# Chunked attention and a gated feed-forward block: copies of v shared between two engines, and two more tiles transposed by DMA

## The chip, the cores and the metric

The kernel runs on one core of a Trainium2 chip. A core has a matrix engine (TensorE, PE in the profile; its weight loads are PEld), a vector engine (VectorE, DVE), an activation engine (ScalarE, ACT), a general one (GpSimd, POOL) and a synchronising one (SyncE, SP), each with a queue of its own that it works through in order. POOL, SP and ACT also issue DMA transfers, which all run on the same 16 DMA engines. Engines wait for each other through semaphores. On-chip memory is SBUF, and matrix products land in PSUM. The metric is the time of one execution on the device in microseconds (us), lower is better.

## The reference: what is computed

Attention over 4 batches, 8 heads, 768 positions and a head size of 64. The positions go in chunks of 32 queries. Each chunk sees 8 memory keys, 16 positions to its left, its own 32 and 8 to its right, 64 keys in all, with a softmax over them. The heads' results are put side by side as rows of 512, and a feed-forward block follows:

```python
for c in range(nc):                       # 24 chunks of 32 queries
    k_full = concat([mem_k, k[l_start:r_end]])
    v_full = concat([mem_v, v[l_start:r_end]])
    a = softmax(scale * q_c @ k_full.T)
    out[chunk] = a @ v_full
x = out as (3072, 512)
y = (relu(x @ w_gate) * (x @ w_val)) @ w_out     # 512 -> 1536 -> 512
```

## The kernel before, in words

**Tiles.** The 3072 rows are 24 tiles of 128 rows, six a batch, each with four chunks. `BLOCKS` gathers the tiles into feed-forward blocks of 2, 2, 2, 4, 4, 4, 4 and 2.

**A tile's attention.** q and k come in by POOL's loads (L254), cast to bf16, into a ring of 18 buffers. They are transposed on PE (`qk_t`, L275) and copied out of PSUM (`qk_copy`), or, for tiles from `LATE_QK` on, by transposing DMA transfers that SP issues (`qk_transfer`, L283): q lands where it is used, k lands in `k_t` and is copied from there into `kT`, where every chunk's keys have the batch's memory keys beside them. Then follow the scores (L309, for which also the next tile's k must be in place), maximum, subtraction, exponent, sum, reciprocal and normalisation (L322 to L352; the exponent on ACT, all else on DVE), the transposition of the probabilities P, on PE (`p_t`, L358) with a copy, or, for tiles from `LATE_P` on, by a transposing transfer from SP (`p_transfer`, L362), the product with v (`values`, L388; L374 and L381 in batch 0), and a copy into the block's xT (`x_copy`).

**v.** For batches 1 to 3, v lies in `v_bd`, two sets used in turn: for each chunk 56 rows of v and 8 of memory, in blocks that are zero elsewhere. POOL loads 32 rows a chunk for each half of the heads (L185). The remaining 24, the upper slots, are the first rows of the next chunk and are copied on chip from one partition group to another: `upper`, 16 copies a batch of 24 x 768 elements, all on DVE (L81, `v_bd<-v_bd`). Rows of memory values come by small transfers (L168), the zeros by ops named `z1` and `z0` on ACT and DVE.

**Feed-forward.** For each block and each of 12 slices of 128 hidden columns: four products for the gate and four for the value (`first`, L407), a relu on ACT (`relu`, L413), a multiplication on DVE (`gate`, L419). Four PSUM buffers are used in turn. Then, per tile, 12 products with w_out (`second`, L432), a copy and a store (`store`, L439).

**The order of the work.** Nothing is scheduled at run time: a planner in the kernel's Python (`schedule`, L682) plays the work through with a cost for each op, and each engine's queue is filled in the order that results. An op has the engines that may do it with a cost on each, its dependencies, a priority tuple (lower is first) and resources that it takes and gives. Whenever an engine is free, in the order POOL, PE, ACT, DVE, SP, the planner walks through that engine's ops by priority and takes the first that is ready. Relus and gates have priority 0, attention ops 1 with the tile's number behind it, feed-forward products 2, some zeroing 3. An `up` op has (1, 6b-1, 9) or (1, 6b+2, 9) for batch b: behind all of tile 6b-1's (or 6b+2's) ops, ahead of the next tile's. Attention ops on PE also keep a margin of 0.4 us (`MARGIN`) behind what they depend on.

For the transposing transfers the planner counts `ISSUE` 1.4 us on SP (and 0.08), then `LAND` 4.5 us for q and k or `LAND_P` 3.0 us for P; a transfer of q or k is put 1.0 us (`SLACK`) behind the landing of its load. The q and k transposes on PE are paced by the feed-forward products (`pace`, from `marks`); those by transfer are paced by the scores of six tiles before (`pace_t`). A transfer issued while the load queue is busy puts that queue 1.1 us back in the plan.

**Memory keys.** `new_batch` (L259) takes one of two q/k buffer sets and fills the memory keys of a batch into all its chunks, one copy on DVE (L263). It stands at tile 6b-2, after that tile's q has been transposed.

Of the kernel before, what the change touches and what calls it, by code (L numbers as in the profile page):

```python
# [14 lines left out]
ACT = mybir.ActivationFunctionType  # L15
# [4 lines left out]
def kernel(  # L20
# [23 lines left out]
    TPB = S // 128  # L44
# [8 lines left out]
    BAND0 = 48  # L53
    UT = 3

    LATE_QK, LATE_P = 15, 15

    KEY_RUNS = ((0, CH, 0), (KW, 64, CH), (CH, KW, CTX))
    assert sum(BLOCKS) == NT and NMEM == 8 and D == 64 and H == 8
# [130 lines left out]
    def upper(b, par, i0, i1, eng):  # L190

        x = v_bd[b % NSET].rearrange("p h c d -> p (h c) d")
        d = slice(D * par, D * par + D)
        copy(eng, x[64 * par + CH:64 * par + CTX, i0:i1, d], x[64 * par:64 * par + CTX - CH, i0 + 1:i1 + 1, d])
# [64 lines left out]
    def new_batch(b):  # L259
        qT[b] = kvpool.tile([128, HP, S], BF16, name="qT")  # L260
        kT[b] = kvpool.tile([128, HP, NCH, KW], BF16, name="kT")
        src = kmemT[:, b]
        nc.vector.tensor_copy(  # L263
            kT[b][:, :, :, 16:16 + NMEM],
            bass.AP(tensor=src.tensor, offset=src.offset,
                    ap=[src.ap[0], [NMEM, HP], [0, NCH], [1, NMEM]]))
# [180 lines left out]
    ops, loads = {}, []  # L447
# [3 lines left out]
    def op(key, eng, fn, deps=(), prio=(0,), take=(), give=(), after=()):  # L451
        ops[key] = dict(eng=eng, fn=fn, deps=list(deps), prio=prio, take=list(take), give=list(give),
                        after=list(after))
# [31 lines left out]
    op("vm0", {"DVE": 0.5}, lambda e: nc.vector.tensor_copy(vmem_0, vmem_f), [("vml", 1.8)], prio=(1, 0, 4.5))  # L485
    for b in range(B):
        op(("new", b), {"DVE": 0.4}, lambda e, b=b: new_batch(b), ["kmc"], take=["kv"],
           prio=(-4.5,) if b == 0 else (1, TPB * b - 2, 0), after=[("t", TPB * b - 2, 0)] if b else [])


    seq = [(blk, m) for g0, g1 in GROUPS for blk in range(2) for m in range(g0, g1)]
# [28 lines left out]
    for a in range(NT):  # L520
        b, t = divmod(a, TPB)
# [60 lines left out]
    for rank, (blk, m) in enumerate(seq):  # L582
        n = BLOCKS[blk]
# [34 lines left out]
    for b in range(1, B):  # L618
        for n in range(2 * HP):
            hp, par = divmod(n, 2)  # L620
            for m in range(TPB // UT):
                i0 = NCH * hp + 4 * UT * m
                i1 = min(i0 + 4 * UT, HP * NCH - 1)
                op(("up", b, n, m), {"DVE": 0.1 + 64 * 0.5e-3 * (i1 - i0)},
                   lambda e, b=b, par=par, i0=i0, i1=i1: upper(b, par, i0, i1, engine[e]),
                   [("vl", b, par)], (1, TPB * b - 1 + UT * m, 9), (), (), [("v", TPB * b - 7)] if b > 1 else [])

# [51 lines left out]
    def timed(d):  # L679
        return isinstance(d, tuple) and len(d) == 2 and isinstance(d[1], float)  # L680

    def schedule():  # L682
        done, started, times = {}, set(), [0.7]
        free = {e: 0.7 for e in ("PE", "ACT", "DVE", "SP", "POOL")}
        queue_end, flying, gives = 0.0, [], [(WARM + 0.15, "fps")]
        room["fps"] -= 1
        heapq.heappush(times, WARM + 0.15)
        todo = {e: [] for e in free}
        order, n_load = [], 0
        names = lambda o: [d[0] if timed(d) else d for d in o["deps"]] + o["after"]  # L690
        missing = {k: len(set(names(o))) for k, o in ops.items()}
        users = {}
        for k, o in ops.items():
            for d in set(names(o)):
                users.setdefault(d, []).append(k)

        def offer(k):
            for e in ops[k]["eng"]:
                bisect.insort(todo[e], (ops[k]["prio"], k), key=lambda x: x[0])

        for k in ops:
            if not missing[k]:
                offer(k)

        def ready(o, t, margin=0.0):
            if any(d not in started for d in o["after"]):
                return False
            for d in o["deps"]:
                d, lag = d if timed(d) else (d, 0.0)
                if d not in done or done[d] + lag + margin > t + 1e-9:  # L710
                    return False
            return all(room[r] >= o["take"].count(r) for r in o["take"])

        while len(started) < len(ops) + len(loads):
            t = heapq.heappop(times)
            while times and times[0] <= t + 1e-9:
                heapq.heappop(times)
            for g in [g for g in gives if g[0] <= t + 1e-9]:
                gives.remove(g)
                room[g[1]] += 1  # L720
            flying = [f for f in flying if f > t]
            moved = True
            while moved:
                moved = False
                for e in ("POOL", "PE", "ACT", "DVE", "SP"):
                    if free[e] > t + 1e-9:
                        continue
                    if e == "POOL":
                        if n_load == len(loads):
                            continue  # L730
                        o = loads[n_load]
                        if len(flying) >= 8 or not ready(o, t):
                            continue
                        n_load += 1
                        key = o["key"]
                        if o["n"]:
                            end = t + 0.62 + 0.27e-3 * o["n"]
                            queue_end = max(queue_end, end + 0.8) + o["work"]
                            flying.append(queue_end + 1.0)
                            done[key] = queue_end + (1.2 if n_load < 8 else 2.4 if n_load < 45 else 6.0 if key[0] == "vl" else 4.0)  # L740
                        else:
                            end = done[key] = t + max(o["work"], 0.6)
                        fn = o["fn"]
                    else:
                        o = None
                        for _, key in todo[e]:
                            late_pe = e == "PE" and t > 36.0 and ops[key]["prio"][0] == 1
                            if ready(ops[key], t, MARGIN if late_pe else 0.0):
                                o = ops[key]
                                break  # L750
                        if o is None:
                            if e == "PE" and 1.3 < t < WARM:
                                order.append((t, lambda: idle_product(256)))
                                free[e] = t + (0.213 if t < 9.0 else 0.11)
                                heapq.heappush(times, free[e])
                            elif e == "PE" and t <= 1.3:
                                heapq.heappush(times, 1.31)
                            continue
                        for x in o["eng"]:
                            todo[x].remove((o["prio"], key))  # L760
                        d = o["eng"][e]
                        d, lat = d if isinstance(d, tuple) else (d, d)
                        d *= (1.8 if e == "PE" and t < 8.0 and key[0] in ("t", "p", "sh", "f") else 1.0)
                        end = t + d
                        done[key] = end + 0.25 if e == "PE" else t + lat + 0.08

                        if queue_end > t:
                            queue_end += 1.1 if e == "SP" and key[0] in ("t", "pc") else 0.7 if key[0] == "oc" else 0.0
                        fn = lambda o=o, e=e: o["fn"](e)
                        for g in o["give"]:  # L770
                            g, lag = g if isinstance(g, tuple) else (g, 0.0)
                            gives.append((done[key] + lag, g))
                            heapq.heappush(times, done[key] + lag)
                    for r in o["take"]:
                        room[r] -= 1
                    started.add(key)
                    for k in users.get(key, ()):
                        missing[k] -= 1
                        if not missing[k]:
                            offer(k)  # L780
                    order.append((t, fn))
                    free[e] = end
                    for x in (end, done[key], done[key] + 0.2, done[key] + 1.5, done[key] + MARGIN):
                        heapq.heappush(times, x)
                    moved = True
            assert times, [k for k in ops if k not in started][:20]
        return order

    for _, fn in schedule():
        fn()  # L790
# [30 lines left out]
```

## Time and profile before

| | us |
|---|---|
| median of 3 runs | 245.17 (244.69 to 246.42) |
| profiled execution | 246.7 |
| its span | 244.9 |
| PE busy | 235.3 |
| DVE busy | 154.0 |
| ACT busy | 122.0 |
| POOL busy | 77.7 |
| copies of v's upper slots on DVE, 48 | 18.3 |

The span runs from the first to the last instruction of the program that the profiler recorded. A timeline line has the start in us from the span's start, the duration, the engine, the line of the kernel (L79 and L81 are the helper `copy`, on ACT and DVE), the operation, and the tile written, an arrow, the tiles read; "x4" counts instructions that were merged; a bracket gives the idle time of the engine just before and what ended it. Instructions of one engine overlap at their ends, so that the step from start to start is the time that one costs its queue. Two engines' names with a q (SPq, ACTq, POOLq) stand for the part that issues transfers. A table by windows gives each engine's busy time in a stretch.

### The profile page before, as it was taken

The numbers are of one execution on the slowest core, as the hardware profiler recorded it, in microseconds if no ns is written. First come the engines' busy times: TensorE is split into PE (matmuls) and PEld (weight loads), VectorE is DVE, ScalarE is ACT, GpSimd is POOL, SyncE is SP. The second block draws the span as 40 slices with busy tenths as digits, with TensorE's granted clock in tenths as the row PEclk, the third lists the DMA queues.
The fourth block names the chain that finished last, engine by engine and source line by source line (L and its number), as shares of the span: only waits on it lengthen the run. The fifth ranks groups of instructions, "written<-read, shape, count | busy, mean of one in ns | idle before, by whom it ended". The sixth has DMA issues, their size and how long they took to land.

```text
span 244.9 us, 6549 instructions
## 1 busy us (share of the span) xinstructions
PE 235.3 (96%) x2706; PEld 140.5 (57%) x2706; DVE 154.0 (63%) x313; ACT 122.0 (50%) x271; POOL 77.7 (32%) x102
## 2 busy tenths in 40 slices
PE   7898999999889999899999999999999999999994
PEld 4576887884379644454544544554445444444873
DVE  5664867977979649988648999995432034310430
ACT  7577778693365336755335655354331233312432
POOL 8975679215984099038250000000000000000000
PEclk9999999999999999999999999999999999999999
DMA  6999999999999999999993121443001210002102
GB/s 71 172 178 203 201 163 151 185 130 124 195 180 169 90 139 119 113 159 128 109 226 60 35 42 29 133 122 48 0 0 45 86 43 0 3 35 93 45 0 86
DMA packets 96413, 25.17 MB, mean 103 GB/s; under 512 B 87424, under 2 KB 93312, under 8 KB 96384
## 3 DMA queue, kind: packets, MB, share of 16 engines
q0 software_dynamic: 76128, 14.65, 85.9%
q1 hardware_dynamic: 16656, 3.82, 15.2%
q10 hardware_dynamic: 3600, 6.29, 7.4%
q8 instruction: 21, 0.34, 0.7%
q14 instruction: 8, 0.07, 0.1%
HBM read 28.55 MB, written 6.29 MB: 142 GB/s over the span
## 4 chain that ended last, share of the span: by engine, by line
PE 63%; DMA 18%; DVE 8%; POOL 5%; issue 3%; ACT 2%; ACTq 0%; POOLq 0%; DVEq 0%
PE out_ps L432 21%; PE g_ps L407 19%; PE v_ps L407 18%; DMA v_bd<-in_v_dram 8%; DMA qk_p<-in_q_dram 6%; DMA w_gate_sb<-in_moe_w_gate_dram 4%; DVE v_bd L81 3%; PE xT_ps L388 2%; PE s_ps L309 1%; DVE gvT L419 1%; POOL v_n L199 1%; DVE dif L329 1%; POOL qk_p L227 1%; DVE mx L322 1%; PE pT_ps L358 1%
## 5 line engine op out<-in xcount | busy, mean ns | idle before, releaser
L419 DVE TENSOR_TENSOR gvT<-v_ps,g_relu 128x256 f16<-128x256 f32 (+1 forms) x96 | 52.8, 553 | 55.5 <-PE v_ps L407 40.4
L407 PE MATMUL v_ps<-xT,w_val_sb 128*128 128x256 f16 (+1 forms) x384 | 78.2, 326 | 0.0
L407 PE MATMUL g_ps<-xT,w_gate_sb 128*128 128x256 f16 (+1 forms) x384 | 78.1, 326 | 0.0
L413 ACT ACTIVATE g_relu<-g_ps 128x256 f16<-128x256 f32 (+1 forms) x96 | 46.8, 490 | 50.3 <-PE g_ps L407 49.1
L432 PE MATMUL out_ps<-w_out_sb,gvT 128*128 128x512 f16 (+2 forms) x300 | 66.0, 371 | 0.0
L407 PEld LDWEIGHTS <-w_gate_sb 128*128 128x128 f16 x384 | 36.3, 98 | 23.7
L407 PEld LDWEIGHTS <-w_val_sb 128*128 128x128 f16 x384 | 36.0, 98 | 21.7 <-issue 0.2
L432 PEld LDWEIGHTS <-gvT 128*128 128x128 f16 x300 | 27.9, 98 | 29.5
L79 ACT COPY o_sb<-out_ps 128x512 f32<-128x512 f32 (+2 forms) x25 | 14.2, 568 | 36.6 <-PE out_ps L432 28.5
L337 ACT ACTIVATE p_exp<-dif 128x256 f16<-128x256 f32 (+2 forms) x72 | 19.6, 337 | 11.9 <-DVE dif L329 11.4
L81 DVE COPY v_bd<-v_bd 24x768 f16<-24x768 f16 (+1 forms) x48 | 18.3, 423 | 3.8 <-DMA v_bd<-in_v_dram 3.3
L254 POOL DMA_DIRECT2D qk_b<-in_q_dram x18 | 16.3, 904 | 8.9 <-DMA v_bd<-in_v_dram 5.7
L322 DVE TENSOR_REDUCE mx<-s_ps 128x8 f32<-128x512 f32 x24 | 16.5, 686 | 4.1 <-PE s_ps L309 3.6
L254 POOL DMA_DIRECT2D qk_b<-in_k_dram x18 | 16.3, 904 | 5.4 <-DMA w_out_sb<-in_moe_w_out_dram 4.0
L341 DVE TENSOR_REDUCE sm<-p_exp 128x8 f32<-128x512 f16 x24 | 16.3, 678 | 2.0 <-ACT p_exp L337 1.9
L352 DVE TENSOR_TENSOR p_n<-p_exp,rinv 128x512 f16<-128x512 f16 x24 | 16.5, 686 | 0.3
L329 DVE TENSOR_TENSOR dif<-s_ps,mx 128x512 f32<-128x512 f32 x24 | 16.4, 682 | 0.2
L168 POOL DMA_DIRECT2D v_bd<-vmem x16 | 10.5, 664 | 14.5 <-DMA v_bd<-in_v_dram 13.1
L185 POOL DMA_DIRECT2D v_bd<-in_v_dram x12 | 11.0, 928 | 11.4 <-DVE gvT L419 10.6
L79 ACT CAST xT<-xT_ps 128x512 f16<-128x512 f32 x16 | 9.4, 584 | 8.2 <-PE xT_ps L388 6.5
L388 PEld LDWEIGHTS <-v_bd 128*128 128x128 f16 x288 | 9.8, 96 | 4.0 <-DVE v_bd L81 0.7
L141 PE MATMUL idle_ps<-idle 128*128 128x256 bf16 x69 | 10.7, 302 | 1.1 <-DVE warm L475 1.1
(56 smaller groups left out, 170.7 us busy)
## 6 DMA issues: line engine op xcount, KB each, us to landing
out_dram<-o_sb ACTq DMA_DIRECT2D x23, 256.0 KB
qk_b<-in_k_dram POOLq DMA_DIRECT2D x18, 128.0 KB, 7.5
qk_b<-in_q_dram POOLq DMA_DIRECT2D x18, 128.0 KB, 7.5
v_bd<-in_v_dram POOLq DMA_DIRECT2D x6, 384.0 KB, 12.5
w_out_sb<-in_moe_w_out_dram POOLq DMA_DIRECT2D x2, 768.0 KB, 11.5
qk_p<-in_k_dram POOLq DMA_DIRECT2D x3, 256.0 KB, 5.4
qk_p<-in_q_dram POOLq DMA_DIRECT2D x3, 256.0 KB, 6.8
v_n<-in_v_dram POOLq DMA_DIRECT2D x6, 128.0 KB, 6.5
```

Source lines behind the costliest of these rows:

```text
L79: nc.scalar.copy(o, i)
L81: eng.tensor_copy(o, i)
L254: nc.gpsimd.dma_start(qk_b[a, i], bass.AP(tensor=x.tensor, offset=x[b, 0, 128 * t, 0].offset, ap=[[D, 128], [S * D, H], [1, D]]))
L322: nc.vector.reduce_max(SM[a, "mx"], s4, axis=AX.X)
L329: nc.vector.tensor_tensor(out=SM[a, "dif"].rearrange("p (m r) a s -> p r m a s", r=2), in0=S_ps.pop(a).rearrange("p r (m a) s -> p r m a s ...
L337: nc.scalar.activation(p[:, :, :, s0:s0 + k1 - k0], dif[:, :, :, k0:k1], ACT.Exp, scale=SCALE)
L341: nc.vector.reduce_sum(SM[a, "sm"], SM[a, "p"], axis=AX.X)
L352: nc.vector.tensor_tensor(out=P_n[a], in0=SM.pop((a, "p")), in1=rinv_b, op=ALU.mult)
L407: nc.tensor.matmul(ps, lhsT=w[:, f, 128 * m:128 * m + 128], rhs=xTs[blk][:, f, :], start=(f == 0), stop=(f == NFC - 1))
L413: nc.scalar.activation(st["r", m], st.pop((0, m)), ACT.Relu)
L419: nc.vector.tensor_tensor(out=st["gv"][:, m, :], in0=st.pop((1, m)), in1=st.pop(("r", m)), op=ALU.mult)
L432: nc.tensor.matmul(st["o", t, c], lhsT=st["gv"][:, m, 128 * t:128 * t + 128], rhs=w_out_sb[:, m, c[0]:c[1]], start=(m == 0), stop=(m == ND ...
```

## The change

Five edits:

- `LATE_QK` and `LATE_P` go from 15 to 13, so that q, k and P of tiles 13 and 14 are transposed by transfers from SP. The k tiles pass through `k_t` and a copy from SBUF.
- The `up` ops may run on ACT (cost 0.16 us + 0.9 ns x 64 for each chunk) as well as on DVE (0.1 us + 0.55 ns x 64, where it was 0.5).
- The planner, as it walks through an engine's ops, notes whether an op of higher priority that is not ready would be ready 0.3 us later (`soon`). If so and the first ready op is an `up` or a `z0`, the engine takes nothing at that moment.
- `new_batch` for batches 2 and 3 may stand from the scores of tile 6b-5 on, with priority (1, 6b-5, 8). Batch 1 keeps its place.
- With tiles 13 and 14 no longer transposed on PE, their q and k are paced by the scores of tiles 7 and 8 and not by the feed-forward products.

```diff
-    LATE_QK, LATE_P = 15, 15
+    LATE_QK, LATE_P = 13, 13
...
         op(("new", b), {"DVE": 0.4}, lambda e, b=b: new_batch(b), ["kmc"], take=["kv"],
-           prio=(-4.5,) if b == 0 else (1, TPB * b - 2, 0), after=[("t", TPB * b - 2, 0)] if b else [])
+           prio=(-4.5,) if b == 0 else (1, TPB * b - 2, 0) if b == 1 else (1, TPB * b - 5, 8), after=[("t", TPB * b - 2, 0) if b == 1 else ("s", TPB * b - 5)] if b else [])
...
-                op(("up", b, n, m), {"DVE": 0.1 + 64 * 0.5e-3 * (i1 - i0)},
+                op(("up", b, n, m), {"ACT": 0.16 + 64 * 0.9e-3 * (i1 - i0), "DVE": 0.1 + 64 * 0.55e-3 * (i1 - i0)},
...
                         o = None
+                        soon = False
                         for _, key in todo[e]:
                             late_pe = e == "PE" and t > 36.0 and ops[key]["prio"][0] == 1
                             if ready(ops[key], t, MARGIN if late_pe else 0.0):
-                                o = ops[key]
+                                o = None if soon and key[0] in ("up", "z0") else ops[key]
                                 break
+                            soon = soon or ready(ops[key], t + 0.3)
```

## The prediction

> **What bounds the kernel now.** I read the page's busy times and slices first, then the PE timeline, then the waits, then SP's and DVE's timelines around the tiles that the change touches.
>
> ```profile
> PE 235.3 (96%) x2706; PEld 140.5 (57%) x2706; DVE 154.0 (63%) x313; ACT 122.0 (50%) x271; POOL 77.7 (32%) x102
> ...
> DMA  6999999999999999999993121443001210002102
> ```
>
> PE is busy in 96% of the span at a granted clock of 1.00. Matmuls overlap in the records, so I checked by start to next start: four 512-column products of the feed-forward part start 0.86 to 0.87 us apart in the last 60 us and in most groups before. From 25 us on PE runs work that has to be done, with few holes; the end moves by what leaves PE's queue and by the holes that open or close. DMA is full (nine tenths) to slice 22, about 135 us, and almost empty after.
>
> The holes are few. The table of windows gives PE 12.24 of 14.00 us in 60:74 and 25.23 of 26.00 in 87:113, and a full count in the other stretches from 25 to 240: 1.76 + 0.77 = 2.53 us in all. In the PE timeline:
>
> ```profile
> 100.19 0.55 PE L388 MATMUL xT_ps<-pT,v_bd 128*128 128x32 f16 x16
> 100.60 0.38 PE L275 MATMUL qk_ps<-ident_b,qk_b 128*128 128x128 bf16 x4
> 100.82 1.03 PE L407 MATMUL v_ps<-xT,w_val_sb 128*128 128x512 f16 x4
> 102.62 0.38 PE L275 MATMUL qk_ps<-ident_b,qk_b 128*128 128x128 bf16 x4 [0.78 <-ACT xT L79]
> 102.84 1.03 PE L407 MATMUL g_ps<-xT,w_gate_sb 128*128 128x512 f16 x4
> ...
> 117.10 0.38 PE L358 MATMUL pT_ps<-band,p_n 128*128 128x128 f16 x4
> 117.32 1.46 PE L432 MATMUL out_ps<-w_out_sb,gvT 128*128 128x512 f16 x6
> ```
>
> The reader sees that a group of four transposes takes 0.22 us to the next start, and that the hole of 0.78 us stands in front of one. By the order of tiles (L275 comes twice a tile, k one tile ahead) that one is tile 13's k; 117.10 is tile 13's P. The holes of 60:74 (0.42, 1.04, 0.30) come from DVE:
>
> ```profile
> 59.40 1.57 DVE L81 COPY v_bd<-v_bd 24x768 f16<-24x768 f16 x4 [1.55 <-DMA v_bd<-in_v_dram]
> ...
> 61.00 0.69 DVE L322 TENSOR_REDUCE mx<-s_ps 128x8 f32<-128x512 f32 x1
> ...
> 61.72 0.78 DVE L81 COPY v_bd<-v_bd 24x768 f16<-24x768 f16 x1
> ...
> 62.54 0.69 DVE L329 TENSOR_TENSOR dif<-s_ps,mx 128x512 f32<-128x512 f32 x1
> ```
>
> Tile 7's scores were done at 58.1, its maximum starts at 61.00: DVE stood at a copy whose rows landed at 59.4, then did four copies.
>
> **Part 1: tiles 13 and 14 leave PE.** Six groups of four transposes go (q, k, P of two tiles): 6 x 0.225 = 1.35 us of PE. The hole of 0.78 stands at one of them and goes with it: the product behind it (102.84) needs a PSUM buffer that the relu at 98.44 freed. Taken: -1.35 - 0.78. Six PSUM copies (0.4 on DVE, 0.6 on ACT) go as well, two SBUF ones come (0.61 on ACT, 0.28 on DVE): nothing on the path.
>
> In their place SP issues six more transposing transfers, and here are the new waits. Engines work in the order that the planner wrote; an instruction whose data lands later than assumed holds up all behind it. The planner allows a transfer 1.48 us of issue, then 4.5 (q, k) or 3.0 (P) to landing. SP's timeline, beside the trace's semaphore records of landing:
>
> ```profile
> 73.54 1.32 SPq L283 DMA_TRANSPOSE k_t<-qk_b  x1
> 75.42 1.75 SPq L283 DMA_TRANSPOSE qT<-qk_b  x1
> ...
> 90.86 1.20 SPq L283 DMA_TRANSPOSE qT<-qk_b  x1
> ...
> 111.69 1.20 SPq L283 DMA_TRANSPOSE k_t<-qk_b  x1
> 112.98 1.25 SPq L283 DMA_TRANSPOSE qT<-qk_b  x1
> ```
>
> They landed at 83.28, 86.46, 98.15, 118.81 and 123.59: 9.7, 11.0, 7.3, 7.1 and 10.6 us after issue. The nine P transfers, all after 139 us, took 2.4 to 4.2.
>
> *P of tile 13.* Its normalisation ends at 115.54 now; without the pacing of tile 13's and 14's transposes by the feed-forward order (`pace`) it comes some us sooner. Either way it lies where DMA is full: the rows of v for batch 3 are issued at 108 and land to 121.6. The planner puts tile 13's values product 4.9 us behind the normalisation (1.48 + 3.0 + MARGIN 0.4), and behind it in PE's queue stands all of PE's work. If the transfer takes as long as the empty-DMA ones, at most 4.2, no wait; as long as the slowest full-DMA one, 10.6, 5.7 us. I take 7.3, the row at 90.86, because it too had no transfer of its own queue in front of it: SP now waits at this transfer, so the ones of tiles 20 to 22 that ran at 105 to 116 come after it. +2.4. Tile 14's P waits for the same traffic at a later place in the order and is covered by the delay already taken.
>
> *k and q of tiles 13 and 14.* SP can start them when their loads land (k 13 at 68.96). The copy out of k_t has 1.0 + 1.48 + 4.5 = 7.0 us from there in the order, plus the 2 us that the holes before 72.6 made all later work late; the rows say 9.7. Wait: 0 to 0.7 on ACT or DVE, in front of relus and gates. With four PSUM buffers in turn a relu of the 512-column blocks may be 2.0 us late (three products of 0.86 minus 0.6), one of the 256-column blocks 0.7. So 0 now, up to 0.7.
>
> *The loads behind them.* Three transfers in 77.6 to 86.1 stretched the second half of batch 2's v rows: the first half took 2.45 us behind the load before it (76.15 to 78.6), the second landed at 85.6, not near 81.5, so some 1.3 us for each transfer. Four more make 5.3. DVE did the copies of that half 3.7 us after landing (89.13), so they would come 1.6 us too early; a gate may be late by 1.9 (2.6 minus 0.7), but tile 10's softmax stands there too. 0 to 1.6; I take +0.5. The k transfer of tile 17 landed at 103.07 and its copy on ACT began at 103.09: no slack at all, with the relu's 2.0 behind it.
>
> **Part 2: upper copies shared.** 48 copies, 18.3 us on DVE. ACT's price is not in the trace for 24x768; ACT copies of 128x512 and 128x1536 f32 took 617 and 1461 ns, so 0.82 ns an element and about 0.83 us for 768 (estimate). A third to a half moved is 13 to 20 us of ACT, which is idle for 47% of 60:74 and 41% of 87:113; beside that it hides, and a relu held up by 0.83 is inside the 2.0, outside by 0.1 in the 256-column blocks: at worst four relus, 0.4 us. The gain is in 60:74: copies after 60.97 no longer go ahead of tile 7's softmax (0.78 at 61.72, 1.4 at 65.20 to 66.9). But the landing at 59.4 stays, and the next late thing is tile 6's values product, which needs all four copies of that half. Between 0 and 1.76 I take a third, -0.6. The lookahead rule also holds zeroing back (done by 53.5, its load issued at 68.8: 15 us of cover).
>
> **Part 3: memory keys early.** Two copies of 0.36 us move to where DVE is 88% busy. At most 0.4 us, taken as nothing.
>
> **Sum.** -1.35 - 0.78 - 0.6 + 2.4 + 0.5 = +0.2 us. The profiled execution took 246.7 with a span of 244.9; the median of the runs is 245.17, with 244.69 to 246.42. I put the difference on the median: **245.4**. 1% (2.5 us) is about what a measurement of this kernel can tell from no change.
>
> **Rivals.** *The transfers land in time (faster).* Then only the savings count: 245.2 - 1.35 - 0.78 - 0.6 = **242.4**. For it: loads for tiles 16 to 21 land before 111, and five transfers now queue behind P 13, so DMA may be emptier than the rows. Against it: not one of the rows between 73 and 117 landed in under 6.3 us. Chance 0.2. [...]
>
> *Transfers at their slowest (slower).* Place: tile 13's values product on PE. Price: 10.6 - 4.9 = 5.7 in place of 2.4, and 1.6 in place of 0.5 at the v rows: 245.2 - 2.73 + 7.3 = **249.8**. It decides from a landing of 9.6 us on, where the sum passes +2.5. For it: five rows issued between 93 and 113 took 9.5 or more. Against: the queue in front of this transfer is shorter. Chance 0.3.
>
> *The sharing does little.* If DVE still takes nearly all copies, or the landing alone made the holes, the -0.6 goes: **246.0**. Chance 0.1.
>
> *The forecast*: 0.4.
>
> **Range.** Low: the fast rival's 242.4. High: the slow rival's 249.8. Below lies closing all of 60:74 with no wait, above a second wait of the same kind. Faster by over 1%: the fast rival less a share that ends within 1%, 0.16. Slower by over 1%: 0.32. Within: 0.52.
>
> **What would show it.** L275 with 56 products and L358 with 52, L283 and L362 with 11 k, 11 q and 11 P transfers, the hardware queue q1 with 544 packets more for each of six. Right: a hole of some 2 us in PE in front of an L388 group around 113 to 122, released by a transfer, and none at 102. Wrong: no hole there (fast rival), or ACT or DVE idle on `k_t` or `v_bd` between 75 and 110 with PE idle behind it; or holes in 60:74 that are larger than before, from copies on ACT that stand in front of relus.

## Result: 10 us slower, and the profile after

The changed kernel takes 255.61 us (median of six runs, 253.33 to 257.35) beside 245.19 us for the kernel before (244.57 to 246.69): a ratio of 1.038, 95% interval 1.033 to 1.043. One of the six executions (257.35) counts as a slow one and is left out of the ratio; the median of the other five is 254.62. Its profiled execution took 256.6 us with a span of 254.8 us, 9.9 us more than the span before.

The page of the kernel after, busy times, slices and the queue of the transposing transfers (packets, MB, share):

```profile
PE 238.3 (94%) x2682; PEld 140.4 (55%) x2682; DVE 144.9 (57%) x289; ACT 139.8 (55%) x291; POOL 77.6 (30%) x102
...
PEclk9999999999999997999989999999999999999999
DMA  7999999999999999999999541232000210003102
...
q1 hardware_dynamic: 19920, 4.61, 18.4%
```

PE has 24 instructions fewer, six groups of four transposes, and yet 3 us more busy time. PEclk, all nines before, has one slice of seven and one of eight. q1 went from 16656 to 19920 packets, 544 for each of six transfers. So the kernel does what the diff says. The loss stands in two places, which the table by windows shows (window, length, busy time of PE, PEld, DVE, ACT and POOL, then PEclk, DMA share, GB/s), first two rows of the kernel before, then three of the kernel after:

```profile
87.00:113.00 26.00, 25.23 (x297) 12.86 (x296) 22.82 (x45) 15.42 (x35) 15.43 (x18) 1.00 2.01 129
...
125.00:150.00 25.00, 25.00 (x349) 12.18 (x347) 21.87 (x42) 14.05 (x33) 0.76 (x1) 1.00 0.46 63
```
```profile
60.00:74.00 14.00, 12.78 (x211) 8.25 (x210) 11.23 (x25) 10.71 (x22) 13.40 (x16) 1.00 2.11 173
87.00:113.00 26.00, 22.75 (x269) 11.43 (x267) 18.05 (x39) 16.59 (x32) 11.99 (x14) 0.93 1.87 115
...
125.00:150.00 25.00, 21.10 (x283) 10.04 (x282) 18.21 (x37) 18.90 (x39) 3.97 (x5) 0.93 1.19 125
```

In 60:74 PE gained 0.54 us on the 12.24 of the kernel before. In 87:113 it lost 2.5, in 125:150 3.9, and in both the granted clock fell to 0.93.

**The first hole.** Timelines of the kernel after, ACT, DVE and PE:

```profile
89.92 0.60 ACT L413 ACTIVATE g_relu<-g_ps 128x512 f16<-128x512 f32 x1 [0.47 <-DVE v_bd L81]
95.25 1.56 ACT L79 COPY v_bd<-v_bd 24x768 f16<-24x768 f16 x2 [4.74 <-DMA v_bd<-in_v_dram]
...
90.07 0.41 DVE L81 COPY kT<-qk_ps 128x512 bf16<-128x512 bf16 x1
95.25 0.35 DVE L81 COPY v_bd<-v_bd 24x768 f16<-24x768 f16 x1 [4.77 <-DMA v_bd<-in_v_dram]
```
```profile
96.38 1.02 PE L407 MATMUL v_ps<-xT,w_val_sb 128*128 128x512 f16 x4 [3.17 <-DVE gvT L419]
97.49 1.86 PE L407 MATMUL g_ps<-xT,w_gate_sb 128*128 128x512 f16 x4
...
101.22 1.03 PE L407 MATMUL g_ps<-xT,w_gate_sb 128*128 128x512 f16 x4
```

ACT and DVE both stand for 4.7 us at an upper copy of the third batch, and end their wait at the same moment: the landing of v's rows, second half, at 95.2 (85.4 before). Relus and gates are queued behind, the four PSUM buffers fill, and PE waits 3.17 us. Then four products take 1.86 us where they take 1.03 later: 427 ns from start to start in place of 216. The granted clock stands at 0.50 from 97.30 to 100.71; half of these 3.4 us, 1.7, is lost. Counted from where the next product would have started, the hole is 3.3 us; with the half-rate stretch 3.3 + 1.7 = 5.0 us.

**The second hole.** SP's and PE's timelines:

```profile
120.50 1.21 SPq L362 DMA_TRANSPOSE pT<-p_n  x1
...
123.14 1.25 SPq L362 DMA_TRANSPOSE pT<-p_n  x1
```
```profile
125.67 0.82 PE L432 MATMUL out_ps<-w_out_sb,gvT 128*128 128x512 f16 x3
128.86 0.50 PE L388 MATMUL xT_ps<-pT,v_bd 128*128 128x32 f16 x14 [2.37 <-DMA pT<-p_n]
130.89 0.22 PE L388 MATMUL xT_ps<-pT,v_bd 128*128 128x32 f16 x2 [1.53 <-issue]
130.96 2.28 PE L432 MATMUL out_ps<-w_out_sb,gvT 128*128 128x512 f16 x6
```

P of tile 13 was issued at 120.50 and landed at 128.81; its values product waits 2.37 us. Then 1.53 us pass inside the product with no releaser that the profile shows, and six products take 2.28 us in place of 1.46; the granted clock is 0.50 again from 131.44 to 134.85. Together 2.4 + 1.5 + 1.7 = 5.6 us.

**The balance.** The planner's times, as the kernel's code computes them, have no idle time on PE after 25.7 us in either kernel, and end 1.44 us earlier after the change: the removed transposes. The trace ends 2.2 us behind the plan before, 13.4 us after; of these 11.2 us the two places hold 10.6. -1.4 + 11.2 = 9.8, and the spans differ by 9.9.

### The profile page after: what moved, and what is told of

It is laid out like the page before. It is cut to its first block, busy times and chain, and to the rows that moved or that the text cites. A ratio compares the mean times of both kernels' runs of the same rounds, so it can differ in the third digit from the quotient of the medians.

```text
span 254.8 us, 6503 instructions
## 1 busy us (share of the span) xinstructions
PE 238.3 (94%) x2682; PEld 140.4 (55%) x2682; DVE 144.9 (57%) x289; ACT 139.8 (55%) x291; POOL 77.6 (30%) x102
## 3 DMA queue, kind: packets, MB, share of 16 engines
q1 hardware_dynamic: 19920, 4.61, 18.4%
## 4 chain that ended last, share of the span: by engine, by line
PE 53%; DMA 30%; POOL 6%; DVE 3%; ACT 3%; issue 3%; ACTq 0%; DVEq 0%; POOLq 0%
DMA v_bd<-in_v_dram 17%; PE g_ps L407 17%; PE v_ps L407 17%; PE out_ps L432 16%; DMA qk_p<-in_q_dram 6%; DMA w_gate_sb<-in_moe_w_gate_dram 4%; DMA pT<-p_n 3%; PE xT_ps L388 2%; ACT v_bd L79 2%; POOL v_bd L185 1%; POOL v_n L199 1%; DVE gvT L419 1%; POOL qk_p L227 1%; PE s_ps L309 1%; DVE sm L341 1%
## 5 line engine op out<-in xcount | busy, mean ns | idle before, releaser
L407 PE MATMUL g_ps<-xT,w_gate_sb 128*128 128x256 f16 (+1 forms) x384 | 79.2, 329 | 0.2
L432 PE MATMUL out_ps<-w_out_sb,gvT 128*128 128x512 f16 (+2 forms) x300 | 67.1, 376 | 0.0
L79 ACT COPY v_bd<-v_bd 24x768 f16<-24x768 f16 (+1 forms) x25 | 20.0, 817 | 6.1 <-DMA v_bd<-in_v_dram 5.3
L168 POOL DMA_DIRECT2D v_bd<-vmem x16 | 10.3, 651 | 24.6 <-DMA v_bd<-in_v_dram 19.6
L79 ACT CAST xT<-xT_ps 128x512 f16<-128x512 f32 x19 | 11.0, 585 | 11.3 <-PE xT_ps L388 9.3
L388 PE MATMUL xT_ps<-pT,v_bd 128*128 128x32 f16 x288 | 9.9, 177 | 3.9 <-DMA pT<-p_n 2.4
```

Of the source, the lines that this page charges most:

```text
L79: nc.scalar.copy(o, i)
L388: nc.tensor.matmul(ps[:, hp, r], lhsT=v_bd[b % NSET][:, hp, 4 * t + g, :], rhs=x[:, hp, r], start=True, stop=True)
L407: nc.tensor.matmul(ps, lhsT=w[:, f, 128 * m:128 * m + 128], rhs=xTs[blk][:, f, :], start=(f == 0), stop=(f == NFC - 1))
L432: nc.tensor.matmul(st["o", t, c], lhsT=st["gv"][:, m, 128 * t:128 * t + 128], rhs=w_out_sb[:, m, c[0]:c[1]], start=(m == 0), stop=(m == ND ...
```

## The experiments

Each is timed beside the kernel before on the same chip, whose median in the four batches was 245.6 to 245.9 us; all ratios are to it, with a 95% interval. Kernels from different batches are best compared by their ratios.

### The change taken apart

Sharing, the rule `soon` and early memory keys alone: the changed kernel with

```diff
-    LATE_QK, LATE_P = 13, 13
+    LATE_QK, LATE_P = 15, 15
```

> Kernel after with both limits back at 15: sharing, lookahead and early memory keys alone. Theory (the six added transfers make the loss, by a landing of v's rows near 95 us and by P of tile 13): no hole over 1 us in PE after 85, the second half of batch 2's rows lands near 85 as before, 245.2 within 1.5 us. Rival (copies on ACT make the loss: two engines stand at the landing and relus with them): a hole of some 3 us near 90 stays, 248 to 250.

The limits alone: the kernel before with 13, 13.

> Kernel before with both limits at 13 and nothing else. Without the early memory keys the q and k transfers of tiles 13 and 14 stand behind tile 10's q in the planner's order, but SP runs ahead of it and may start them at their loads' landing (69 us) all the same. Theory: the rows of v land near 95 and DVE, which has all the copies, holds up the gates: PE hole of 3 to 4 us near 92, one of some 4 us at tile 13's values product, 253 to 256. Rival (ACT copies make it): only the hole at tile 13's P, 248 to 250.

q and k alone (13, 15), and P alone (15, 13), with the rest of the change:

> Kernel after with the limit for P back at 15: q and k of tiles 13 and 14 by transfer, their P on PE. Theory: the hole near 92 (3.3 us, and about 1.7 us of products at half rate behind it) stays, those at 126 and 129 (4.2 and 1.7) go for tiles 13 and 14 but may come back in part at tile 15's P: 249 to 251. Rival (one cause for both holes, in P's transfers): no hole at 92, 245.

> Kernel after with the limit for q and k back at 15: only P of tiles 13 and 14 by transfer. Theory: rows of v land near 85, no hole at 92; a hole of 2 to 5 us at tile 13's values product (its transfer takes 7 to 10 us, the order gives it 4.9): 247 to 250. Rival (P's transfers are slow only because the q and k transfers crowd them): no hole over 1 us, 244 to 245.

| kernel | us | ratio |
|---|---|---|
| sharing alone | 245.03 | 0.999 (0.996 to 1.001) |
| limits alone | 254.56 | 1.037 (1.034 to 1.041) |
| sharing, q and k | 255.52 | 1.040 (1.036 to 1.045) |
| sharing, P | 249.32 | 1.015 (1.010 to 1.020) |

Sharing alone, the same windows:

```profile
60.00:74.00 14.00, 13.24 (x231) 9.11 (x230) 10.54 (x23) 10.48 (x25) 11.96 (x14) 1.00 2.14 192
87.00:113.00 26.00, 25.54 (x316) 13.39 (x315) 23.12 (x44) 18.78 (x38) 14.65 (x19) 1.00 1.89 142
```

PE gains 1.0 us in 60:74 and waits for no row in 87:113, though 21 of 48 copies run on ACT. The whole loss comes from the limits. It is not additive: q and k alone, expected at 249 to 251 us, cost what all costs. My reading is that a stall in one place lets transfers land that would have stalled PE in the next; no run separates this. With q and k alone the values product of tile 15, whose P was a transfer before too, waits 3.8 us; with the limits alone it is that of tile 13 (what waited, for what, us in all, times, longest):

```profile
PE xT_ps L388 <- DMA pT<-p_n: 4.8, 1, 4.8
```

### Only the traffic

The kernel before in its own order, with four transfers that nobody reads in front of tile 15's first:

```diff
+        if (a, i) == (15, 1):
+            for n, key in enumerate([(13, 1), (13, 0), (14, 1), (14, 0)]):
+                nc.sync.dma_start(qk_p[n % 2, n // 2][:, 0:HP, :], qk_b[key].rearrange("p h d -> p (h d)"), transpose=True)
```

> Kernel before, order untouched, with four more transposing transfers on SP in front of tile 15's: q and k of tiles 13 and 14 into buffers that nothing reads any more (their transposes on PE stay, so this is pure traffic). Theory (traffic): the second half of batch 2's rows of v lands at 91 to 95 and not at 85, DVE stands at its copies, PE hole of 1 to 4 us near 92, 247.5 to 251. Rival (not the traffic, but what waits in the new order): rows late, no hole over 1 us, 245 to 246.

250.15 us, ratio 1.017 (1.012 to 1.022). The order of the work is that of before, and DVE stands at an upper copy again:

```profile
91.65 0.35 DVE L81 COPY v_bd<-v_bd 24x768 f16<-24x768 f16 x1 [3.04 <-DMA v_bd<-in_v_dram]
```

So four more transfers in front, with the order as it was, cost 4.3 us there; the holes on PE are of 1.4 us and less, and the clock stays at 1.00. What the changed kernel loses beyond that, some 5 us by the ratios, is left for P's transfers and for its order.

### Mending one wait in the order

The changed kernel with the third batch's upper copies planned 9 us later:

```diff
-                   [("vl", b, par)], (1, TPB * b - 1 + UT * m, 9), ...
+                   [(("vl", b, par), 9.0 if b == 2 else 0.0)], (1, TPB * b - 1 + UT * m, 9), ...
```

> Kernel after; in the planner only, batch 2's upper copies are held to 9 us behind the landing that it counts for the rows. Theory: ACT and DVE no longer stand at the landing (95 us), so the hole near 92 (3.3 us) and the half-rate products behind it (1.7) go, the one at tile 13's P stays: 250 to 251.5. Rival (the late rows hold up more than the copies' place): 254 or more.

With P's transfer planned at 8.5 us in place of 3.0 (`LAND_P`):

> Kernel after with the planner's landing of a P transfer at 8.5 us in place of 3.0. The plan itself then has 2.1 us of idle PE at tile 13's values product. Theory: PE no longer waits in the middle of the w_out products at 126 to 131 (4.2 us and 1.7 of half rate), 2 to 3 us remain, the hole near 92 stays: 251.5 to 253.5. Rival (the P transfers only follow what was late already): 255 to 257.

With the scores of tiles 13 and 14 held to the feed-forward products, as the transposes that they lost had been:

```diff
+    def pace_s(a):
+        if a not in (13, 14):
+            return []
+        blk = block_of[a]
+        at = begun[blk] - LEAD + STEP * (a - starts[blk])
+        return [key for c, key in marks if c <= at][-1:]
...
-           ["kv"] if last else [], [("s", a - 1)] if a else [])
+           ["kv"] if last else [], ([("s", a - 1)] if a else []) + pace_s(a))
```

> Kernel after with the scores of tiles 13 and 14 held to the same feed-forward products as their q transposes were before; the transfers stay where they are. Theory (traffic and a planner that counts too little for landing): hole near 92 stays, hole at tile 13's P stays at 2 to 5 us, 252 to 256. Rival (the attention running ahead of the feed-forward part is what puts P into full DMA): the hole at 126 to 131 goes or falls under 1.5 us, 249 to 251.

They took 254.89 (1.037, 1.029 to 1.045), 258.36 (1.050, 1.043 to 1.056) and 255.19 us (1.036, 1.029 to 1.043): none came near the kernel before, and the planned landing of P made it worse. The first two miss what the theory expected of them (250 to 251.5 and 251.5 to 253.5); the third came as expected. PE of the first:

```profile
123.69 0.55 PE L388 MATMUL xT_ps<-pT,v_bd 128*128 128x32 f16 x16 [2.85 <-DMA pT<-p_n]
124.17 0.35 PE L309 MATMUL s_ps<-kT,qT 64*32 64x64 bf16 x32
124.45 3.71 PE L432 MATMUL out_ps<-w_out_sb,gvT 128*128 128x512 f16 x9
133.09 0.61 PE L388 MATMUL xT_ps<-pT,v_bd 128*128 128x32 f16 x16 [4.93 <-DMA pT<-p_n]
```

The hole at 92 is gone, and tiles 13 and 14 wait 7.8 us for their P in its place: P of tile 14 took 15.0 us. Work that came earlier met the same late DMA landings. In the second the plan itself has 2.1 us of idle time, and its scores wait 4.4 us elsewhere. In the third P of tile 13 took 10.3 us and cost 4.9. With the rows landing at 93 to 95 in these three, one wait mended was a wait moved.

### The rows of v ahead of the transfers

The loads of batch 2's rows are put on POOL ahead of the loads of q and k for tiles 13 and on, so that the added transfers are issued behind them; the whole change, then with P from tile 15 on, then with both limits at 15:

```diff
-        for a, i in late[5 if b == 1 else 9 + 12 * (b - 1):21 + 12 * (b - 1)]:
+        for a, i in late[5 if b == 1 else 14 if b == 2 else 33:14 if b == 1 else 33 if b == 2 else 45]:
```

> The changed kernel; only the order of the loads on POOL differs: the rows of v and of the memory values for the third batch are issued ahead of the loads of q and k for tiles 13 and on, so that the four added transposing transfers come behind the rows. Theory (what the four transfers cost is paid where they stand in front of the rows): the rows' second half lands by 84 us in place of 95.2, no PE hole of over 1 us between 90 and 101, and the hole at the values product of tile 13 (P's transfer, 7 to 10 us) stays: 249 to 252 us. Rival (the DMA is full in this stretch in any order, so what is moved back is late in place of the rows): q and k of tiles 13 and 14 land later than their scores allow, a hole of 2 to 4 us appears there, and the time stays at 254 to 257 us.

> As the run with the rows of the third batch ahead, and P by transposing transfers only from tile 15 on, as in the kernel before; q and k stay at tile 13. Theory: neither hole is left, the planner's 0.94 us of removed transposes show: 243.5 to 246 us. Rival (full DMA in any order): holes at the scores of tiles 13 to 16 or at the values products of tiles 15 and 16, 250 to 255 us.

> The shared copies with both limits at 15, as in the kernel before, and the third batch's rows of v ahead of the loads of q and k for tiles 13 and on. Theory: the rows land before 84 us, no hole is left after 85, time 244 to 245.5 us, within 0.5% of the run with the shared copies alone (245.0). Rival (the loads of q and k of tiles 13 to 16 become late in their place): a hole of 1 to 3 us at the transposes or scores of tiles 13 to 15, 246 to 248 us.

| kernel, rows ahead | us | ratio |
|---|---|---|
| 13, 13 | 251.97 | 1.023 (1.018 to 1.028) |
| 13, 15 | 253.38 | 1.030 (1.023 to 1.037) |
| 15, 15 | 245.95 | 1.001 (0.998 to 1.004) |

The rows now land at 74 to 75, no engine waits for them and the hole at 92 is gone, as expected; the first kernel's largest holes stand at the values products of tiles 13 (1.0 us) and 15 (2.7). That moving them costs nothing measurable by itself is seen with 15, 15. The second was expected at 243.5 to 246 and missed. Its tiles 14 to 17 have their scores at 112 to 123, 15 us sooner than in the kernel before, because q and k of tiles 13 and 14 no longer wait for a place among PE's products and the tiles behind follow; so P of tiles 15 to 17 is issued between 122 and 130, where the transfers take 6.8 to 9.3 us (2.4 at 143), and PE waits for two of them. And DVE stands at the copy of tile 16's k, whose transfer the plan has at 4.5 us and which took 7.9, with the sum and the next maximum behind it:

```profile
98.27 0.68 DVE L419 TENSOR_TENSOR gvT<-v_ps,g_relu 128x512 f16<-128x512 f32 x1
101.05 0.29 DVE L81 COPY kT<-k_t 128x512 bf16<-128x512 bf16 x1 [2.10 <-DMA k_t<-qk_b]
...
101.86 0.68 DVE L341 TENSOR_REDUCE sm<-p_exp 128x8 f32<-128x512 f16 x1
```

### The order mended for what the DMA does

With rows ahead and 13, 15, three steps: the scores paced as above; the landing of q and k planned at 9 us; and P of tiles 13 and 14 by transfer after all.

```diff
-    ISSUE, LAND, SLACK, LAND_P = 1.4, 4.5, 1.0, 3.0
+    ISSUE, LAND, SLACK, LAND_P = 1.4, 9.0, 1.0, 3.0
```

> As the run with the rows of the third batch ahead and only q and k of tiles 13 and 14 by transposing transfers, which took 253.4 us; in addition the scores of tiles 13 and 14 are held to the feed-forward products, as the transposes that they replace were. Theory (what is left of the loss there is that tiles 14 to 17 run 13 us ahead of their order in the kernel before, so that P of tiles 15 to 17 is transferred at 122 to 137, where the DMA is full and a transfer takes 7 to 9 us): P of tile 15 is issued after 135, takes under 4 us, the holes at 128 and 133 and the half-rate products behind them go: 245 to 248 us. Rival (the loss is the DMA time of the four added transfers wherever the tiles run): holes of over 2 us remain between 115 and 140, 251 to 254 us.

> As the paced run, and the planner counts 9 us in place of 4.5 from the issue of a transposing transfer of q or k to its landing, the time that they take between 68 and 130 us. Theory (in-order engines stand at a copy that was placed for an earlier landing: the second vector-engine wait for k at 99 to 101, with 3 us of holes at the scores and the values product of tile 12 behind it): those holes go too and the time is 0.5 to 3 us below that of the paced run, 244 to 246 us. Rival (where the copy stands in the order makes no difference): the same as the paced run within 0.5 us.

> As the run before it, with P of tiles 13 and 14 by transposing transfers too, counted at 3 us as in the changed kernel: this is the whole change with the rows ahead, the scores paced and q and k counted at 9 us. Theory (P of tile 13 is issued at 114 to 118 beside the fourth batch's rows and takes 7 to 10 us, against 4.9 that the order allows): one hole of 2.5 to 5 us at the values product of tile 13, with up to 1.7 us of half-rate products: 248 to 251 us. Rival (P was late only for the other transfers and delays): no hole over 1 us, 243.5 to 246 us.

| kernel, rows ahead | us | ratio |
|---|---|---|
| 13, 15 | 253.38 | 1.030 (1.023 to 1.037) |
| and paced | 247.35 | 1.008 (1.004 to 1.011) |
| and `LAND` 9 | 245.16 | 0.999 (0.996 to 1.001) |
| and `LATE_P` 13 | 248.32 | 1.009 (1.005 to 1.013) |

All three times came as the theory said. Pacing takes off about 5.5 us by the ratios (the first row is of another batch): P of tile 15 is issued at 137.4 and takes 2.5 us. `LAND` at 9 takes off 2.2. In the paced kernel both engines still stand for k, DVE for tile 16's and ACT for tile 17's:

```profile
102.02 0.29 DVE L81 COPY kT<-k_t 128x512 bf16<-128x512 bf16 x1 [2.60 <-DMA k_t<-qk_b]
106.83 0.62 ACT L79 COPY kT<-k_t 128x512 bf16<-128x512 bf16 x1 [4.95 <-DMA k_t<-qk_b]
```

With `LAND` 9 these copies have moved behind the landings (tile 16's k lands at 104.70, its copy starts at 106.37), and neither engine waits for a transfer of k there. DVE:

```profile
98.00 0.69 DVE L419 TENSOR_TENSOR gvT<-v_ps,g_relu 128x512 f16<-128x512 f32 x1
98.61 0.68 DVE L329 TENSOR_TENSOR dif<-s_ps,mx 128x512 f32<-128x512 f32 x1
100.13 0.69 DVE L419 TENSOR_TENSOR gvT<-v_ps,g_relu 128x512 f16<-128x512 f32 x1 [0.84 <-PE v_ps L407]
```

The four transfers of q and k of tiles 13 and 14 are all still there, at 6.6 to 8.2 us each, and cost nothing that can be measured; nor do they gain: the 0.94 us that the plan saves is within 1%. `LAND` 9 holds for all tiles by transfer, and no run has it with both limits at 15, so what it would do for the kernel before by itself is not shown. P of tile 13 puts 3.2 us back. PE of the last one:

```profile
113.69 6.63 PE L432 MATMUL out_ps<-w_out_sb,gvT 128*128 128x512 f16 x30
122.02 0.57 PE L388 MATMUL xT_ps<-pT,v_bd 128*128 128x32 f16 x16 [1.69 <-DMA pT<-p_n]
```

P was issued at 114.5 and landed at 122.0, beside the fourth batch's rows. The hole of 1.7 us is smaller than the 2.5 to 5 expected, and no half rate follows in this execution; four of the ten executions show a granted clock of 0.991 to 0.993. The kernel with `LATE_P` 15 is 10 us faster than the changed one and level with the one before; none of the kernels is measurably faster than that.

### Without the fourth batch's rows

The changed kernel without those four loads (the fourth batch is then computed with the second batch's rows of v):

```diff
     def load_v_rows(b, par, s0, s1, c0, c1):
+        if b == 3:
+            return
```

> The changed kernel without the four loads of v's rows for the fourth batch (left out; the products of that batch then run on the second batch's rows, at the same cost). Theory (P's transfer of tile 13 waits behind these rows in the DMA): P of tile 13 takes 3 to 5 us in place of 8.3, the hole at its values product around 126 to 131 goes, with the half-rate products behind it, and the time falls by 4 to 6 us to 249.5 to 252 us; the hole at 92 to 97 stays. Rival (P is slowed by the transposing transfers of q and k on its own queue, or by the normalisation being late): P still takes 7 us or more, the hole stays, 254 to 257 us.

252.41 us, ratio 1.024 (1.017 to 1.031). The time and P lie between the two expectations. The profile is of the fastest of the four executions, 249.59 us, at a granted clock of 1.00; two of the others (251.92 and 252.95 us) show 0.993. In the profile P of tile 13 took 5.6 us, and the second hole shrank to pieces of 0.7, 1.1 and 0.3 us with no half rate behind them. The first stayed, with 1.7 us in place of 3.2 and no half rate either, so a part of this execution's gain is not the rows'. With the DMA quiet, from 145 us on, a P transfer of the changed kernel took 2.4 us at the least; of the 5.9 us that tile 13's took beyond that in the changed kernel, leaving out the rows takes 2.7 away. The rest is not theirs: P was issued here at 116.68, and the k transfer before it in its own queue landed at 119.90. P of tile 14 still took 7.5 us beside the transfers of q and k in that queue.

## Why the prediction was wrong

- **PE's savings (-1.35 - 0.78).** Right as far as the plan shows it: it is 1.44 us shorter, the counts of instructions are as listed, and no hole stands at 102.
- **Sharing (-0.6).** Right in kind: 0.54 us gained in 60:74 after the change, 1.0 with sharing alone. A copy on ACT took 0.82 us on average, as estimated, and 25 of 48 went there, so the rival by which the sharing does little did not come true. In the time of the whole kernel the gain is too small to measure (0.999).
- **P of tile 13 (+2.4).** The wait itself was 2.37 us, and P took 8.3 us where 7.3 was taken. That the two waits agree is luck in part: PE came to the product some 1 us later than the 4.9 us of the order. The normalisation ended at 120.5, 5 us later than before and not sooner as forecast; the first hole stands in front of it. What failed was that a wait costs only its length. The 1.53 us inside the product and the half-rate products made 5.6 us of it. In the last paced kernel, whose profiled execution has neither, its span is 2.0 us above that of the kernel with `LAND` 9 (246.4 and 244.4); the medians, with four executions at a lower clock, differ by 3.2.
- **The loads behind (+0.5, at most 1.6).** This is the step that failed most. I priced an added transfer at 1.3 us of the load stream, from the three of the kernel before. From the issue of the last rows to their landing it is 12.2 to 13.4 us with three transposing transfers before or among them (the kernel before, sharing alone, P alone), 18.0 with six (limits alone), and 20.4 to 22.9 with seven (the changed kernel, q and k alone, the three that mended one wait, the one without the fourth batch's rows, and, with the 20.4, the four transfers that nobody reads). Against the 12.9 of the kernel before that is 1.7 us for each of three more, 1.9 to 2.5 for each of four. With the rows ahead and no transfer among them it is 8.8 to 10.2, with fewer loads in front too. The rows of the changed kernel came 10 us late instead of 5.3, and the copies on both engines stood for them: 5.0 us in place of 0.5. Where they came 5.3 us late, as computed (limits alone, 90.7), DVE stood 1.45 us for them and PE was idle for 2.0 us between 95 and 110 (0.8 before); how much of that is the rows' is not separated. The prediction named this very sign (ACT or DVE idle on `v_bd` between 75 and 110 with PE idle behind it), but gave it a price that could not decide.
- **q and k of tiles 13 and 14 (0, at most 0.7).** For these tiles it held: in the changed kernel only the copy of tile 14's k waited, 0.56 us on ACT at 83.47. What had no term are the k transfers that come behind them in SP's queue. DVE waited 4.5 us for tile 15's k at 87.95, while PE ran products with w_out without a hole; in the paced kernel tiles 16 and 17 are the ones waited for, and planning their landings takes 2.2 us off. The prediction saw that tile 17's copy had no slack and gave it no price.
- **"Tile 14's P waits for the same traffic and is covered".** In the changed kernel itself it held: its P landed at 132.57 and its values product, at 134.76, did not wait. It fails where the place moves: with the upper copies later it waited 4.9 us. That tiles lose their place among PE's products was seen, but only as an earlier P of tile 13. It brings tiles 14 to 17 forward into the full DMA, which is worth about 5.5 us once the rows are out of the way. In the changed kernel pacing alone gained nothing; P of tile 13 then took 10.3 us.
- **Rivals.** The slow one had the mechanism and the place, but both its prices together (7.3 us) stop at 249.8 us: a half-rate term and a late landing of 10 us were in none of the bounds. The fast one did not come true: P of tile 13 took 8.3 us, and in the trace its transfer moved nothing beside the load queue at first. From just after 118.50 to 124.48 the load queue moved 6278 packets and q1 none, though P of tile 13 had been issued at 120.50; its first moved at 124.48, 4.0 us after issue, as the bulk of the fourth batch's rows came to an end. In the kernel before, the transfer issued at 73.54 beside the load queue moved its first packet at 77.62, 4.1 us after issue, and the one issued at 139.62, alone, at 140.80, 1.2 us after. What held P's transfer back is not shown.

What stays open: what an added transfer takes from the rows more exactly than 1.7 to 2.5 us, and what the 1.53 us inside the values product wait for (without the fourth batch's rows the same two instructions come 0.73 us late).

## What to carry to other kernels

Where an order is fixed ahead, the landing of a transfer decides what moving work to it from a full engine is worth: here the plan gained 1.44 us, and P of tile 13, planned at 4.5 us from issue to landing (1.48 + 3.0), took 8.3 and its place cost 5.6 us. Read the landings in the stretch where the transfer will run, not in the quiet one (6.4 to 15.0 us here against 2.4 to 4.4), and put that time into the plan. Look at what the new transfers stand in front of before asking what they cost by themselves, and at what loses its place in the order when its old engine lets it go. Where one wait was mended here and the time stayed, the next landing had taken it over; the source, here the place of the loads, had to be mended first.

## What was not expected of the hardware

PE's products ran at half rate after a hole: 427 ns from start to start in place of 216, with PEclk below nine in the slice. By the idle times that the profiles of the kernels run here give before PE's instructions, from 85 us on, it came after all ten holes of 2.3 us or more (2.33 to 4.93), after one of the four between 1.85 and 2.07, and after none that was shorter and stood alone. In the changed kernel it lasted 3.4 us and cost 1.7 us at both places, from 97.30 to 100.71 and from 131.44 to 134.85, at a granted clock of 0.50.

A transposing transfer of 128 x 512 took 2.4 to 4.4 us from issue to landing with the DMA quiet (after 143 us) and 6.4 to 15.0 us where it was issued between 69 and 117 us, in the kernels before and after.
